# A sparse-attention block with two expert layers on one core: the rows of the next expert are split ahead of the weight conversion

## The chip, the cores and the metric

The kernel runs on one core of one Trainium2 chip. The metric is the device time of one execution in microseconds (us). The kernel before has a median of 1108.11 us over three runs (1107.55 to 1112.84). The core has five engines that each run their own instructions in order and meet through semaphores: TensorE (PE: matmuls; PEld is its weight load), VectorE (DVE), ScalarE (ACT), GpSimd (POOL) and SyncE (SP, which here only issues DMA transfers).

## The reference, cut to what matters

```python
x   = attention(q, k, v)             # 4 x 8 heads x 576 x 64, causal window 128, a bias by distance
x   = x.transpose(0, 2, 1, 3).reshape(2304, 512)
lg  = x @ w_gate + log1p(exp(x @ w_noise)) * noise      # 8 experts
top2, weight = the two largest of lg, softmax over them
for e in range(8):                   # layer 1: w1[e] 512 x 1024, w2[e] 1024 x 512
    rows = tokens that chose e
    out[rows] += weight * (relu(x[rows] @ w1[e]) @ w2[e])
h   = relu(out @ w_in)               # layer 2: w_in 512 x 2048, w_out 2048 x 512
return (h * h) @ w_out
```

All of it is float32. The kernel reaches that precision on PE by splitting a number into a high and a low part (type fp32r) and adding three products: high by high, high by low, low by high. So every operand of an expert matmul must be split on other engines first.

## The kernel before, in words

There are three stages: attention with the routing, the eight experts, and the second layer. The change lies in the experts and at the end of the first of them.

**Experts.** Each expert has at most 630 rows here, in five groups j = 0 to 4 (of 126 or 128 rows), and its weights come in eight blocks f = 0 to 7. A step n = 8e + f is one block of one expert. In PE's order a step is `expert_a(n)`, called a(n) here (12 matmuls into the PSUM tile hA, for the first 374 rows, then 12 into hB, for the rest), then `expert_b(n-1)`, called b(n-1) (15 matmuls that add the previous block to the five results y). T(n) is the time at which a(n) starts. hA has two PSUM buffers, hB has one, so hB of the next step waits until ACT and DVE have emptied this one. That emptying is `relu`: ACT writes the high part, then DVE writes the low part. The DVE half of it is called the relu below.

**What else a step does**, in the order of the code in `experts`:
- `fetch` lets POOL gather the rows of the next expert out of DRAM (group f, by row numbers in the tile `ids`), and lets SP transpose the group before it.
- `load_weights(n+7)` and `load_half(n)` are transfers on SP's queue, which runs in order. A half is one half of a block of the second layer's weights, in float64 bits that have to be made into float32.
- `begin_half` (ACT, line 1092) and `convert_half` (six DVE instructions, lines 1104 to 1109) convert the half that was loaded one step earlier. Together the six are called the conversion. The list HALVES names the steps that load one: 32 in all.
- `split_weights(n+5)`: ACT casts the high part of the weights (line 725, the cast), and POOL subtracts four pieces for the low part (line 729).
- `prepare` makes the next expert's operand: ACT joins two byte planes (line 427) and casts the high part (line 758), and DVE subtracts the low part (line 759, called the split below; the tile is `turned`). Group j is split in step f = j + 3, so group 4 is split in step f = 7, just ahead of the next expert's a.

The engines' order on PE, DVE, ACT and SP is the order of the code. POOL's is chosen by the scheduler, and it is the same in both kernels. The cast of w(n+5) writes into the buffers of w(n-1), so it starts when b(n-1) has ended, which is at T(n+1). Everything that `prepare` has on ACT stands behind that cast.

**Expert 0** is run in two passes (`first_expert`): the first over the 256 rows that are routed early, the second over the rest. In the second pass the rows of expert 1 are fetched and prepared. The row numbers of expert 0's late groups, of experts 1 to 6 and of expert 7 are loaded by three transfers in `settle`. Ahead of expert 1 stands a branch over code for more rows than planned (`overflow`, line 866); it is not taken with these inputs, and every engine jumps over that code.

## Time and profile before

| | |
|---|---|
| median of three runs | 1108.11 us (1107.55 to 1112.84) |
| the profiled execution | 1101.99 us |
| its span | 1100.2 us |
| PE busy in the span | 1036.5 us (94%) |
| DVE, ACT, POOL busy | 534.4, 485.2, 483.5 us (49%, 44%, 44%) |
| chain that ended last | PE 58%, DVE 5%, DMA 4%, issue 3%, POOL 2%, ACT 1% |
| attention and expert 0 | up to 283.3 us |
| experts 1 to 7 | from 283.3 to some 690 us |
| second layer | from there to the end |

PE is the engine to watch. An idle stretch of PE is printed behind the row that ends it, with the instruction that was waited for. [...] Idle time of the other engines matters only where PE waits at its end.

### The profile page before, as it was taken

The page shows a single profiled execution, that of the slowest core. Times are in us where ns is not written, and L with a number is a line of the kernel's source. Part 1 is how long each engine was busy: PE and PEld are TensorE (multiplying, and loading weights), DVE is VectorE, ACT ScalarE, POOL GpSimd, SP SyncE. Part 2 cuts the span into 40 slices and gives each one's busy share as a digit, 9 for nine tenths or more (in the row PEclk, how much of TensorE's full clock was granted, in tenths as well). Part 3 has the DMA queues.
Part 4 walks back from the last instruction along what each step waited for, and adds up shares of the span by engine and source line. Part 5 has one row for each costly group of instructions (what it writes and reads, how often), then busy time and mean ns, then how long its engine had stood idle before and what let it go on. Part 6 is the DMA issues. An engine that isn't in the chain of part 4 may idle for free.

```text
span 1100.2 us, 17058 instructions
## 1 busy us (share of the span) xinstructions
PE 1036.5 (94%) x6264; PEld 931.6 (85%) x6264; DVE 534.4 (49%) x1353; ACT 485.2 (44%) x897; POOL 483.5 (44%) x558
## 2 busy tenths in 40 slices
PE   4798989979899999998999999999999999999998
PEld 3687778869788989897888988899999999999997
DVE  7779687642357576756574421562232322223211
ACT  4678586435345454543453532553333333323322
POOL 5356464434466676665566563322222222222221
PEclk7879898789999999998999999999999999999999
DMA  9999993266495958586767422211212221031101
GB/s 200 173 177 207 192 170 102 79 151 158 129 208 172 212 185 215 192 216 188 185 170 199 113 67 72 72 39 34 73 20 67 48 68 39 10 83 33 29 1 29
DMA packets 204269, 131.43 MB, mean 119 GB/s; under 512 B 123108, under 2 KB 180580, under 8 KB 204176
## 3 DMA queue, kind: packets, MB, share of 16 engines
q1 hardware_dynamic: 195312, 109.39, 42.3%
q0 software_dynamic: 8864, 20.86, 6.9%
q8 instruction: 51, 0.84, 0.3%
q14 instruction: 42, 0.34, 0.1%
HBM read 84.56 MB, written 19.95 MB: 95 GB/s over the span
## 4 chain that ended last, share of the span: by engine, by line
PE 58%; DVE 5%; DMA 4%; issue 3%; POOL 2%; ACT 1%; SPq 0%; POOLq 0%; ACTq 0%; DVEq 0%
PE y L734 30%; PE h L734 18%; PE hA L734 6%; PE hB L734 5%; DMA raw<-in_moe_w_out_dram 2%; DVE turned L759 1%; POOL ring L729 1%; DMA y_dram<-xT,ids 1%; DVE raw L1108 1%; DVE store L1105 1%; DVE store L1106 1%; DMA raw<-in_moe_w_in_dram 1%; DVE raw L1107 1%; POOL first L729 0%; DVE hh L820 0%
## 5 line engine op out<-in xcount | busy, mean ns | idle before, releaser
L1141 POOL TENSOR_TENSOR hh<-relu,hh 128x384 fp32r<-128x384 f32 x96 | 97.2, 1013 | 296.9 <-ACT hh L1140 296.9
L1138 DVE SCALAR_TENSOR_TENSOR relu<-h,relu 128x384 f32<-128x384 f32 x96 | 53.5, 557 | 246.6 <-ACT relu L1137 246.6
L734 PE MATMUL y<-first,hh 128*126 128x512 f32 (+2 forms) x642 | 158.8, 396 | 0.0
L734 PE MATMUL y<-ring,hh 128*126 128x512 f32 (+1 forms) x612 | 151.7, 396 | 0.3 <-POOL hh L1141 0.3
L734 PEld LDWEIGHTS y<-first,hh 128*126 128x126 f32 (+2 forms) x642 | 117.7, 188 | 24.4 <-ACT hh L819 0.3
L734 PEld LDWEIGHTS y<-ring,hh 128*126 128x126 f32 (+1 forms) x612 | 112.9, 189 | 23.7 <-POOL hh L1141 0.8
L1137 ACT ACTIVATE relu<-h 128x384 f32<-128x384 f32 x96 | 47.1, 491 | 192.8 <-PE h L734 192.8
L729 POOL TENSOR_TENSOR first<-raw,first 128x256 fp32r<-128x256 f32 x116 | 97.0, 866 | 68.7 <-ACT first L725 55.6
L729 POOL TENSOR_TENSOR ring<-raw,ring 128x256 fp32r<-128x256 f32 x108 | 93.3, 893 | 52.1 <-ACT ring L725 41.7
L734 PE MATMUL y<-store,hh 128*128 128x512 f32 (+1 forms) x444 | 114.7, 397 | 0.0
L734 PE MATMUL h<-turned,store 128*128 128x384 f32 x552 | 107.4, 337 | 0.0
L734 PEld LDWEIGHTS h<-turned,store 128*128 128x128 f32 x552 | 98.1, 188 | 4.0
L734 PEld LDWEIGHTS y<-store,hh 128*128 128x128 f32 (+1 forms) x444 | 83.7, 190 | 15.3
L820 DVE SCALAR_TENSOR_TENSOR hh<-hA,hh 128x374 fp32r<-128x374 f32 (+3 forms) x76 | 39.8, 523 | 99.6 <-ACT hh L819 99.4
L734 PE MATMUL hA<-turned,first 128*128 128x374 f32 (+3 forms) x444 | 82.0, 335 | 4.2 <-ACTq L866 3.5
L734 PEld LDWEIGHTS hA<-turned,first 128*128 128x128 f32 x444 | 76.7, 194 | 7.9 <-ACTq L866 3.9
L1140 ACT CAST hh<-relu 128x384 fp32r<-128x384 f32 x96 | 49.3, 514 | 69.3 <-DVE relu L1138 65.5
L734 PE MATMUL hA<-turned,ring 128*128 128x374 f32 (+3 forms) x420 | 74.6, 327 | 0.0
L734 PEld LDWEIGHTS hA<-turned,ring 128*128 128x128 f32 x420 | 70.5, 188 | 3.0
L353 ACT ACTIVATE prob<-neg,least 128x256 f32<-128x256 f32 (+2 forms) x144 | 61.4, 473 | 9.3 <-DVE least L346 7.7
L759 DVE TENSOR_TENSOR turned<-x,turned 128x504 fp32r<-128x504 f32 (+2 forms) x41 | 41.1, 1004 | 47.3 <-ACT turned L758 47.1
L359 PE MATMUL ps_pt<-identf,prob 128*128 128x128 f32 (+1 forms) x256 | 49.2, 315 | 14.4 <-DVE den L408 11.4
(202 smaller groups left out, 1952.1 us busy)
## 6 DMA issues: line engine op xcount, KB each, us to landing
raw<-in_moe_w_dram SPq DMA_DIRECT2D x128, 256.0 KB, 3.7
raw<-y_dram SPq DMA_DIRECT2D x18, 512.0 KB, 4.0
raw<-in_moe_w_in_dram SPq DMA_DIRECT2D x16, 512.0 KB, 5.7
raw<-in_moe_w_out_dram SPq DMA_DIRECT2D x16, 512.0 KB, 5.8
vraw<-in_v_dram SPq DMA_DIRECT2D x36, 128.0 KB, 5.5
x_dram<-xn SPq DMA_DIRECT2D x18, 256.0 KB, 3.3
out_dram<-osb SPq DMA_DIRECT2D x36, 128.0 KB, 2.4
qraw<-in_q_dram SPq DMA_DIRECT2D x7, 512.0 KB, 4.9
```

What stands on the lines that cost most here:

```text
L353: self.nc.scalar.activation(u.p[:, a, :u.w], u.neg[:, a, :u.w], AF.Exp, bias=u.least[:, a:a + 1], scale=-1.0)
L359: self.nc.tensor.transpose(u.pt[:n, a, ci, :], u.p[:, a, ci * P:ci * P + n], self.identf)
L729: engine.tensor_sub(w[1][:, c], raw[:, c], w[0][:, c])
L734: self.nc.tensor.matmul(out, a(x), b(y), start=first and i == 0, stop=last and i == 2)
L759: self.nc.vector.tensor_sub(dst[:, 1, :, col:col + n], x[:, :, :n], dst[:, 0, :, col:col + n])
L820: nc.vector.scalar_tensor_tensor(hh[:, 1], ps, 0.0, hh[:, 0], op0=ALU.max, op1=ALU.subtract)
L1105: nc.vector.tensor_scalar(a, a, 3, 0x3FFFFFFF, op0=ALU.logical_shift_left, op1=ALU.bitwise_and)
L1106: nc.vector.scalar_tensor_tensor(a, hi, -0x40000000, a, op0=ALU.bitwise_and, op1=ALU.bitwise_or)
L1137: nc.scalar.activation(r, ps, AF.Relu)
L1138: nc.vector.scalar_tensor_tensor(r, ps, 0.0, r, op0=ALU.max, op1=ALU.mult)
L1140: nc.scalar.copy(hh[:, 0, :], r)
L1141: nc.gpsimd.tensor_sub(hh[:, 1, :], r, hh[:, 0, :])
```

## The change

Five edits: (1) HALVES leaves out the steps f = 7, so that no half is converted in the step f = 0, in which the five results of an expert are copied out; the list still has 32 entries, so it now reaches into expert 7 (steps 56 and 58 instead of ending at step 50). (2) In `experts`, `prepare` stands ahead of `convert_half`. (3) In `first_expert`, `fetch` stands at the head of the loop. (4) There `prepare` has a lag of two blocks and no longer three. (5) The row numbers of expert 0 have a tile of their own.

```diff
-HALVES = [n for n in range(8, 8 * NE) if n % 8 in (0, 2, 3, 5, 6, 7)][:32]
+HALVES = [n for n in range(8, 8 * NE) if n % 8 in (0, 2, 3, 5, 6)][:32]
...
-            in_offset=bass.IndirectOffsetOnAxis(ap=self.ids[:, e, j, 0:1], axis=0))
+            in_offset=bass.IndirectOffsetOnAxis(ap=self.ids_of(e)[:, j, 0:1], axis=0))
...
-        self.ids = self.const.tile([P, NE, 5, 2], I32, name="ids")
+        self.ids0 = self.const.tile([P, 5, 2], I32, name="ids0")
+        self.ids = self.const.tile([P, NE - 1, 5, 2], I32, name="ids")
...
+    def ids_of(self, e):
+        return self.ids[:, e - 1] if e else self.ids0
...
         for f in range(8):
+            self.fetch(1, f + 1)
             if f + 1 < 8:
                 self.expert_a(0, f + 1, (1,))
             self.expert_b(0, (f,), rest)
             if 8 + f < 14:
                 self.split_weights(8 + f, nc.vector if f < 2 else nc.gpsimd)
                 self.load_weights(8 + f + 3)
-            self.fetch(1, f + 1)
-            self.prepare(1, f + 1, 3)
+            self.prepare(1, f + 1)
...
+            if e + 1 < NE:
+                self.prepare(e + 1, f)
             if n - 1 in HALVES:
                 self.convert_half(HALVES.index(n - 1))
-            if e + 1 < NE:
-                self.prepare(e + 1, f)
```

DVE before, from the split of group 4 (step f = 7 of expert 1) to the copies of the results y in step f = 0 of expert 2; the split is the row `turned`, the conversion the six rows with `store` and `raw`:

```order
L759 TENSOR_TENSOR turned<-x,turned 128x4x126
L820 SCALAR_TENSOR_TENSOR hh<-hA,hh 128x374
L820 SCALAR_TENSOR_TENSOR hh<-hB,hh 128x256
L1104 TENSOR_SCALAR store<-store 128x512
L1105 TENSOR_SCALAR store<-store 128x512
L1106 SCALAR_TENSOR_TENSOR store<-raw_6064,store 128x512
L1107 TENSOR_SCALAR raw_6064<-store 128x512
L1108 SCALAR_TENSOR_TENSOR raw_6064<-raw_6064 128x512
L1109 TENSOR_TENSOR store<-store,raw_6064 128x512
L838 COPY xT<-y_5707 126x512
L838 COPY xT<-y_5715 126x512
```

DVE in the changed kernel, the same place (its lines 1108 to 1113 are the conversion):

```order
L759 TENSOR_TENSOR turned<-x,turned 128x4x126
L1108 TENSOR_SCALAR store<-store 128x512
L1109 TENSOR_SCALAR store<-store 128x512
L1110 SCALAR_TENSOR_TENSOR store<-raw_5997,store 128x512
L1111 TENSOR_SCALAR raw_5997<-store 128x512
L1112 SCALAR_TENSOR_TENSOR raw_5997<-raw_5997 128x512
L1113 TENSOR_TENSOR store<-store,raw_5997 128x512
L820 SCALAR_TENSOR_TENSOR hh<-hA,hh 128x374
L820 SCALAR_TENSOR_TENSOR hh<-hB,hh 128x256
L838 COPY xT<-y_5708 126x512
L838 COPY xT<-y_5716 126x512
```

The conversion that stood between the relu of step f = 0 and the copies is gone, and the one that stood ahead of the split now stands behind it, between the split and the relu of the next step.

SP before, in the second pass of expert 0: the transposes of expert 1's rows (`xT<-x`) among the loads of weights:

```order
L705 DMA raw<-in_moe_w_dram 128x4x128
L707 DMA raw<-in_moe_w_dram 128x512
L705 DMA raw<-in_moe_w_dram 128x4x128
L707 DMA raw<-in_moe_w_dram 128x512
L705 DMA raw<-in_moe_w_dram 128x4x128
L707 DMA raw<-in_moe_w_dram 128x512
L785 DMA_TRANSPOSE xT<-x 128x8x128
```

SP in the changed kernel, the same place:

```order
L705 DMA raw<-in_moe_w_dram 128x4x128
L707 DMA raw<-in_moe_w_dram 128x512
L705 DMA raw<-in_moe_w_dram 128x4x128
L707 DMA raw<-in_moe_w_dram 128x512
L785 DMA_TRANSPOSE xT<-x 128x8x128
L705 DMA raw<-in_moe_w_dram 128x4x128
L707 DMA raw<-in_moe_w_dram 128x512
```

Each of the five transposes moves ahead of one pair of loads.

POOL before, with the semaphores that each instruction waits for: the gathers of expert 0's three late groups and the first of expert 1's:

```order
L745 DMA x<-x_dram,ids 128x1024 [waits DMAHW4_49,DMAHW5_49,DMAHW3_49,DMAHW6_49,DMAHW2_49,DMASW6_49]
L745 DMA x<-x_dram,ids 128x1024 [waits DMASW7_49,PE_49,Pool_49]
L745 DMA x<-x_dram,ids 128x1024 [waits DMASW0_49,PE_49]
L745 DMA x<-x_dram,ids 128x1024 [waits DMASW7_49,DMAHW4_49,DMASW1_49,Activation_49]
L745 DMA x<-x_dram,ids 128x1024 [waits DMASW2_49,DVE_49,PE_49]
```

POOL in the changed kernel, the same place:

```order
L745 DMA x<-x_dram,ids_3135 128x1024 [waits DMAHW4_49,DMAHW5_49,DMAHW3_49,DMAHW6_49,DMAHW2_49,DMASW6_49]
L745 DMA x<-x_dram,ids_3135 128x1024 [waits DMASW7_49,PE_49,Pool_49]
L745 DMA x<-x_dram,ids_3135 128x1024 [waits DMASW0_49,PE_49]
L745 DMA x<-x_dram,ids 128x1024 [waits DMASW7_49,DMAHW4_49,DMASW1_49,Activation_49]
L745 DMA x<-x_dram,ids 128x1024 [waits DMASW2_49,DVE_49,PE_49]
```

Only the name of the tile differs; the semaphores are the same, and so are the values that are waited for in the two programs.

## Rows read from the trace of the kernel before

**Rows 1.** Busy time by stretch (experts 1 to 7; after step 40's stall): PE, PEld, DVE, ACT, POOL, clock, DMA

```profile
283.34:690.00 406.66, 395.61 (x2182) 355.30 (x2183) 219.28 (x349) 182.58 (x279) 242.19 (x273) 0.98 0.62 168
...
519.62:523.00 3.38, 3.38 (x14) 3.18 (x15) 0.61 (x2) 0.62 (x2) 0.96 (x1) 0.50 0.69 200
```

**Rows 2.** Timeline of PE, expert 1: start, duration, instruction, [idle before it <- releaser]

```profile
316.35 2.22 PE L734 MATMUL hA<-turned,ring 128*128 128x374 f32 x12
321.03 2.21 PE L734 MATMUL hB<-turned,ring 128*128 128x256 f32 x12 [2.46 <-DVE hh L820]
327.64 2.22 PE L734 MATMUL hA<-turned,first 128*128 128x374 f32 x12
329.70 1.60 PE L734 MATMUL hB<-turned,first 128*128 128x256 f32 x12
334.61 2.22 PE L734 MATMUL hA<-turned,first 128*128 128x374 f32 x12
...
344.51 1.59 PE L734 MATMUL hB<-turned,first 128*128 128x256 f32 x11 [0.59 <-DVE turned L759]
```

**Rows 3.** Timeline of PE, first steps of experts 4 and 5 (32 and 40)

```profile
458.37 1.58 PE L734 MATMUL hB<-turned,first 128*128 128x256 f32 x11 [1.30 <-DVE turned L759]
...
511.84 2.23 PE L734 MATMUL hA<-turned,first 128*128 128x374 f32 x12
...
519.62 2.72 PE L734 MATMUL hB<-turned,first 128*128 128x256 f32 x11 [5.44 <-DVE turned L759]
526.18 2.22 PE L734 MATMUL hA<-turned,ring 128*128 128x374 f32 x12
```

**Rows 4.** Timeline of all engines, one step (14) of expert 1

```profile
327.66 1.05 ACT L725 CAST ring<-raw 128x1024 fp32r<-128x1024 f32 x1 [4.00 <-PE y L734]
...
328.79 3.29 POOL L729 TENSOR_TENSOR ring<-raw,ring 128x256 fp32r<-128x256 f32 x4 [0.36 <-ACT ring L725]
...
329.84 0.60 ACT L758 CAST turned<-x 128x504 fp32r<-128x504 f32 x1
...
330.48 1.00 DVE L759 TENSOR_TENSOR turned<-x,turned 128x504 fp32r<-128x504 f32 x1 [2.49 <-ACT turned L758]
...
331.85 0.41 DVE L820 SCALAR_TENSOR_TENSOR hh<-hB,hh 128x256 fp32r<-128x256 f32 x1
...
332.31 0.43 DVE L1104 TENSOR_SCALAR store<-store 128x512 f32<-128x512 f32 x1
...
335.38 0.69 DVE L1109 TENSOR_TENSOR store<-store,raw 128x512 f32<-128x512 f32 x1
```

**Rows 5.** The split by its line, steps 11 to 63: ns min/median/max, first and last start

```profile
L759 DVE TENSOR_TENSOR turned<-x,turned x30: 676/1203/1231, 319.0 to 632.9; 128x504 fp32r<-128x504 f32 x25, 128x512 fp32r<-128x512 f32 x4, 128x472 fp32r<-128x472 f32 x1
```

**Rows 6.** Timeline of ACT, step 12 of expert 1

```profile
313.56 0.66 ACT L1092 ACTIVATE store<-raw 128x512 f32<-128x512 f32 x1 [4.87 <-DMA raw<-in_moe_w_out_dram]
...
316.30 0.60 ACT L758 CAST turned<-x 128x504 fp32r<-128x504 f32 x1
```

**Rows 7.** Timeline of ACT, DVE and POOL, step 40 (first of expert 5)

```profile
512.80 0.61 ACT L758 CAST turned<-x 128x504 fp32r<-128x504 f32 x1
...
513.15 3.18 DVE L1105 TENSOR_SCALAR store<-store 128x512 int32<-128x512 int32 x1
513.26 2.79 POOL L729 TENSOR_TENSOR first<-raw,first 128x256 fp32r<-128x256 f32 x4
```

**Rows 8.** The branch line 866: instructions by engine's queue, ns min/median/max, first and last start

```profile
L866 ACTq EVENT_SEMAPHORE  x2: 17/17/17, 283.3 to 283.4; - x2
...
L866 PEldq COMPARE_BRANCH  x1: 4625/4625/4625, 278.4 to 278.4; - x1
```

**Rows 9.** Timeline around the branch: PE, POOL, ACT

```profile
281.14 0.99 POOL L839 DMA_INDIRECT y_dram<-xT,ids  x1 [3.27 <-ACT xT L838]
281.23 0.62 ACT L758 CAST turned<-x 128x504 fp32r<-128x504 f32 x1
...
283.34 3.21 PE L734 MATMUL hA<-turned,first 128*128 128x374 f32 x12 [3.49 <-ACTq L866]
```

More of the change, by code (lines that the diff above doesn't have):

```diff
@@ L840, in expert_b @@
                     out=self.y_dram[:, :],
-                    out_offset=bass.IndirectOffsetOnAxis(ap=self.ids[:n, e, j, 1:2], axis=0),
+                    out_offset=bass.IndirectOffsetOnAxis(ap=self.ids_of(e)[:n, j, 1:2], axis=0),
                     in_=ysb[:n], in_offset=None)
@@ L914, in load_ids @@
         rows = self.ids_dram[e * REG + j0 * P:e * REG + j1 * P, :]
-        self.nc.sync.dma_start(self.ids[:, e, j0:j1], rows.rearrange("(j p) o -> p j o", p=P))
+        self.nc.sync.dma_start(self.ids_of(e)[:, j0:j1], rows.rearrange("(j p) o -> p j o", p=P))
+    def ids_of(self, e):
+        return self.ids[:, e - 1] if e else self.ids0
     def early_rows(self):
@@ L965, in settle @@
         src = self.ids_dram.rearrange("(e r) o -> e (r o)", e=NE)[1:NE - 1, :10 * P]
-        nc.sync.dma_start(self.ids[:, 1:NE - 1].rearrange("p e j o -> p e (j o)"),
+        nc.sync.dma_start(self.ids[:, :NE - 2].rearrange("p e j o -> p e (j o)"),
                           src.rearrange("e (p a) -> p e a", a=10))
```

## The prediction

> **What bounds the kernel now.** I read busy time by stretch first. In experts 1 to 7 PE works 395.61 of 406.66 us [rows 1], so at most 11.05 us of idle time can be won there, and whatever the slow clock costs behind a long stall; what comes after is the same code in both kernels. The timeline of PE then says where those 11 us lie. An undisturbed step lasts 334.61 - 327.64 = 6.97 us, and its hB starts 2.06 us after T [rows 2]. Stalls are few, and DVE ends all of them but one. In the first step of an expert PE stops after one matmul of hB and waits for the split of group 4: 0.59 us in step 16 [rows 2], 1.30 in step 32 and 5.44 in step 40 [rows 3]; the first steps of experts 3 and 6 have a row like that of step 16. In step 13 hB waits 2.46 us for the relu of step 12 [rows 2]. [...] The exception stands ahead of expert 1, where PE is idle for 3.49 us until line 866 on ACT's queue [rows 9].
>
> Then I read one quiet step engine by engine [rows 4], with T(14) = 327.64. ACT's cast starts at T, because it waits for PE's b. The high part of the next expert's group is there at T + 2.80 (329.84 + 0.60), the split runs from T + 2.84 to T + 3.84, the relu of hB ends at T + 4.62, and the conversion runs from T + 4.67 to T + 8.43 (3.76 us). The deadline of the relu is the next hB, at T + 6.97 + 2.06 = T + 9.03. So before, the relu has 4.4 us to spare.
>
> **Expert 0's row numbers apart: 0 us.** The gathers wait for the same semaphores at the same values in both programs. The wait that the edit would remove is not there, because the regions of the tile were already told apart.
>
> **Expert 1's rows a step sooner: 0 us for PE, something for POOL.** The gap ahead of expert 1 ends with the jump. PE's compare-and-branch starts at 278.4 and lasts 4625 ns, to 283.0, and ACT's own semaphore rows of that line stand at 283.3 [rows 8]. The last row work on ACT ended at 281.23 + 0.62 = 281.85, before either [rows 9]. When it goes, the jump is late next, and it does not move, because PE's order ahead of it is the same; I take 0 (bounds 0 and 4.5, the second in the rivals). On SP five transposes pass one pair of loads each. The gathered rows they wait for come from POOL instructions that stand far ahead, and the loads behind them wait for a free buffer anyway, so this costs nothing; were a gather late, loads for expert 1's blocks would be late with it. On POOL there is a gain: the scatter of expert 0's results waited 3.27 us for copies on ACT [rows 9] that stand behind a join and a cast for expert 1's rows, which are now done a step earlier. A cast is 0.6 us [rows 9] and the join ahead of it starts with the cast of weights and ends with this one: from 327.66 + 1.05 to 329.84 is 1.1 us at least [rows 4]. So POOL leaves expert 0 some 1.7 us earlier.
>
> [...]
>
> **The split ahead of the conversion.** The split cannot start before ACT's high part, at T + 2.80. Before, DVE used the wait for it to convert. Now the conversion stands behind the split, and the relu behind the conversion. From the same rows: split to T + 3.84, conversion 3.87 + 3.76 = T + 7.63, both relus (331.48 to 332.26, 0.8) to T + 8.4. That is 0.6 us ahead of the deadline where there were 4.4. This holds for four steps in each of six experts (a split followed by a conversion, f = 3, 4, 6, 7): 24 steps. Price of one: 0 if the conversion takes 3.76. POOL's pieces end at 328.79 + 3.29 = T + 4.44, inside the new place of the conversion, and DVE instructions beside POOL are longer: the split takes 676 ns at least and 1203 in the median [rows 5]. One instruction lengthened by 0.5 uses up nearly all of the slack; with all six it would be overdrawn by 2.4. I take 0.1 for each, +2.4 us (bounds 0 and 12, at 0.5 each).
>
> *First steps.* The high part of group 4 is there 512.80 + 0.61 - 511.84 = 1.57 us after T [rows 7, 3], a split beside POOL takes 1.2 [rows 5], and the second matmul of hB would start at T + 2.33. So about 0.5 us of stall stays even with a free DVE, and steps 16, 24 and 48 have no more than that now: 0. Step 32 goes from 1.30 to 0.6: -0.7. Step 56, which had almost no conversions ahead of it, gets them now: +0.5 (bounds 0 and 0.7).
>
> *Step 40.* Ahead of its split stood a conversion in which one instruction took 3.18 us, until POOL's four pieces had ended (513.26 + 2.79 = 516.05) [rows 7]. That conversion now stands behind the split. What delays the split still is the conversion of the step before, which waits for its own split: in step 12, rows of the same kind show the high part ready at 316.90, 2.7 us behind the end of ACT's first part of the conversion, 314.22 [rows 6]. If the late half comes again, I put the stall at 2.2 us and the loss at 3.5: -3.9. Without it the loss is 0.8: -6.6. I take -3.9, since a late transfer of this kind is in the trace.
>
> *Step 13.* This is the opposite case. The half came 4.87 us late, ACT finished its part at 314.22, and the high part of the split followed at 316.90 [rows 6]. DVE could convert in between; now it waits. That is 2.7 us longer for the relu that PE waits for, less the 1.7 by which POOL is earlier: +1.0 (bounds -4.3, the whole loss of 11.29 - 6.97 [rows 2], and +2.7).
>
> **The halves of f = 7 left out.** The six instructions that stood between the relu of f = 0 and the copies go, 3.76 us of DVE. PE did not wait for them. Their place is taken by the conversion from behind the split. 32 conversions stay 32; the last ones move into experts 6 and 7, where PE waits for nothing of theirs: 0.
>
> **Sum.** 0 + 0 + 2.4 - 0.7 + 0.5 - 3.9 + 1.0 = -0.7 us, against the profiled execution's 1101.99 (span 1100.2): 1101.3. The timed median is 1108.11, 6.1 us above the profiled execution, and the same difference gives 1107.4. I predict 1107 us: no change. About 0.5% (5.5 us) is what a measurement of this kernel can tell from none.
>
> **Rivals.**
>
> *Faster: the stalls that DVE ends go.* Speaks for it: a split no longer stands behind a slow conversion, and there is one conversion fewer around the copies. Against it: 0.5 us of each first step is ACT's, and the relu pays. Step 40 -6.6, step 32 -0.7, step 13 wholly gone -4.3, no price in the 24 steps, +0.5: -11; two thirds of it, as some late transfers return: about 1100.5 us. Chance 0.23.
>
> *Faster: the rows, not the jump, hold PE ahead of expert 1.* Then PE goes on at once: 3.49 us, and the first hA at its usual length, 3.21 - 2.22 = 1.0 [rows 9, 2]: -4.5, with the -0.7 about 1103 us. For it: the gap's releaser is printed as ACT. Against it: PE's own branch row. [...] Chance 0.06.
>
> *Slower: the relu becomes the bound.* The mechanism is one: a conversion beside POOL is longer than 4.4 us (9.03 - 3.87 - 0.8), so the relu ends behind T + 9.03, and hB of the next step waits, in up to 24 steps. For it: the slack of 0.6 us, and a split that is usually at its long duration. Against it: POOL's pieces end 0.6 us into the conversion in rows 4. At 0.5 us each it is +12, less 3 of the gains: +9, about 1117 us; it decides from 0.3 us each. Chance 0.21.
>
> [...]
>
> **How the numbers follow.** No change 0.50, the rivals 0.23, 0.06 and 0.21. The branch case lies at the edge of what can be told, so I count it as faster by half: faster 0.27, same 0.52, slower 0.21. The forecast's own range is 1103 to 1112. To hold 8 in 10 it must reach well into both sides: 1099 to 1116.
>
> **What would show it.** In the changed kernel's trace: PE's branch row still some 4.6 us and the gap ahead of expert 1 within 0.3 of 3.49; the split starting right behind ACT's cast and the conversion behind it; the relu of hB ending near T + 8.4 in steps f = 4, 5, 7 and 0; first steps at 0.5 to 0.8 us of stall; step 40 below 3. It is wrong if hB waits for the relu in many steps (slower), if the waits for `turned` all go (faster), or if the gap ahead of expert 1 closes.

## The result and the profile after

The changed kernel takes 1097.07 us in the median of 20 runs (1091.3 to 1105.1), against 1107.69 us for the kernel before on the same chip (20 runs). The ratio is 0.9909, with a 95% interval of 0.9885 to 0.9934: some 10 us faster. The forecast was no change at 1107 us, with a range of 1099 to 1116, so the time fell outside the range on the fast side. What came true is the rival "the stalls that DVE ends go", which was put at 1100.5 us, nearer to its whole sum of -11 us than to the two thirds of it that it took.

The profiled execution took 1095.01 us (span 1093.3, granted clock 0.966 as a share of full speed), 6.98 us less than that of before. Experts 1 to 6, from the first hA of step 8 to that of step 56, are called the stretch below. It went from 631.35 - 283.34 = 348.01 us to 623.75 - 288.23 = 335.52 us: -12.49. Most of the difference to 6.98 lies ahead of the stretch, which began 4.89 us later in this execution. Two executions of either kernel differ as much there (288.23 and 283.69 us in the changed kernel, 283.34 and 292.41 in the one before), so these 4.89 us can't be put down to the change. I compare stretches below, each from one profiled execution, and give the ratio of timed runs beside them.

Busy time in the stretch, of the kernel before and of the changed one (columns as in [rows 1]):

```profile
283.34:631.35 348.01, 337.02 (x1857) 303.30 (x1858) 207.11 (x327) 164.58 (x248) 216.94 (x241) 0.98 0.69 183
288.23:623.75 335.52, 334.36 (x1857) 300.56 (x1858) 186.44 (x306) 163.44 (x246) 202.89 (x239) 0.99 0.66 186
```

In the stretch PE now idles for 335.52 - 334.36 = 1.16 us, where it was 348.01 - 337.02 = 10.99. Of the 12.49 us 9.83 are idle time, and 2.66 are matmuls that took less time (mean granted clock 0.99 instead of 0.98). The timeline of PE shows which stalls went (start, duration, instruction, idle time before it and its releaser):

```profile
288.23 3.26 PE L734 MATMUL hA<-turned,first 128*128 128x374 f32 x12 [3.85 <-ACTq L866]
...
323.66 1.70 PE L734 MATMUL hB<-turned,ring 128*128 128x256 f32 x12 [0.19 <-DVE hh L820]
...
345.11 1.59 PE L734 MATMUL hB<-turned,first 128*128 128x256 f32 x11 [0.16 <-DVE turned L759]
...
513.53 1.57 PE L734 MATMUL hB<-turned,first 128*128 128x256 f32 x11 [0.15 <-DVE turned L759]
```

They answer to [rows 9], [rows 2] (steps 13 and 16) and [rows 3] (step 40). The wait in step 13 fell from 2.46 to 0.19 us, that in step 40 from 5.44 to 0.15, and every first step now waits 0.15 or 0.16. Only the gap ahead of expert 1 stayed. There the rows of the branch line answer to [rows 8]:

```profile
L866 ACTq EVENT_SEMAPHORE  x2: 17/17/17, 288.2 to 288.2; - x2
L866 PEldq COMPARE_BRANCH  x1: 4685/4685/4685, 282.9 to 282.9; - x1
```

Last, one step with a split and a conversion (step 28, T = 426.97), from the timelines of ACT, DVE and PE; it answers to [rows 4]:

```profile
429.27 0.60 ACT L758 CAST turned<-x 128x504 fp32r<-128x504 f32 x1
...
429.90 0.98 DVE L759 TENSOR_TENSOR turned<-x,turned 128x504 fp32r<-128x504 f32 x1 [5.36 <-ACT turned L758]
430.81 0.96 DVE L1108 TENSOR_SCALAR store<-store 128x512 f32<-128x512 f32 x1
...
434.18 0.69 DVE L1113 TENSOR_TENSOR store<-store,raw 128x512 f32<-128x512 f32 x1
434.79 0.54 DVE L820 SCALAR_TENSOR_TENSOR hh<-hA,hh 128x374 fp32r<-128x374 f32 x1
435.25 0.41 DVE L820 SCALAR_TENSOR_TENSOR hh<-hB,hh 128x256 fp32r<-128x256 f32 x1
...
436.01 1.60 PE L734 MATMUL hB<-turned,ring 128*128 128x256 f32 x12
```

This is the order that the prediction walked: high part, split, conversion, relus. Of the six conversion instructions only the first, beside POOL's pieces (they end at 431.48), is long (0.96 where it takes 0.43 alone). The relu ends at 435.66 = T + 8.69, 0.35 us ahead of the hB at 436.01, which does not wait.

### The profile page after: what moved, and what is told of

Read it like the earlier page. It is cut to its first block, busy times and chain, and to the rows that moved or that the text cites. A ratio compares the mean times of both kernels' runs of the same rounds, so it can differ in the third digit from the quotient of the medians.

```text
span 1093.3 us, 17064 instructions
## 1 busy us (share of the span) xinstructions
PE 1033.5 (95%) x6264; PEld 927.8 (85%) x6264; DVE 526.7 (48%) x1353; ACT 483.8 (44%) x897; POOL 472.7 (43%) x558
## 4 chain that ended last, share of the span: by engine, by line
PE 61%; DVE 4%; issue 4%; ACT 2%; DMA 1%; POOL 1%; SPq 0%; ACTq 0%; POOLq 0%
PE y L734 31%; PE h L734 18%; PE hA L734 7%; PE hB L734 6%; DVE turned L759 1%; ACT x L427 1%; DMA y_dram<-xT,ids 1%; DVE store L1108 1%; DVE hh L820 1%; DVE raw L1112 1%; DVE store L1110 1%; DMA raw<-in_moe_w_out_dram 0%; ACT turned L758 0%; DVE raw L1111 0%; DVE store L1109 0%
## 5 line engine op out<-in xcount | busy, mean ns | idle before, releaser
L729 POOL TENSOR_TENSOR first<-raw,first 128x256 fp32r<-128x256 f32 x116 | 92.1, 824 | 73.3 <-ACT first L725 68.6
L729 POOL TENSOR_TENSOR ring<-raw,ring 128x256 fp32r<-128x256 f32 x108 | 85.4, 822 | 60.0 <-ACT ring L725 57.4
L759 DVE TENSOR_TENSOR turned<-x,turned 128x504 fp32r<-128x504 f32 (+2 forms) x41 | 37.9, 926 | 90.3 <-ACT turned L758 90.1
```

Source lines behind the costliest of these rows:

```text
L729: engine.tensor_sub(w[1][:, c], raw[:, c], w[0][:, c])
L759: self.nc.vector.tensor_sub(dst[:, 1, :, col:col + n], x[:, :, :n], dst[:, 0, :, col:col + n])
```

## Experiments

"Stretch" is the time from the first hA of step 8 to that of step 56, in the profiled execution of each kernel. Ratios are against the kernel before, timed on the same chip.

| kernel | stretch, us | ratio (95%) |
|---|---|---|
| before, two executions | 348.01, 352.76 | 1 |
| changed, two executions | 335.52, 337.57 | 0.9909 (0.9885 to 0.9934), 0.9921 (0.9882 to 0.9960) |
| e2: order alone | 356.58 | 1.0101 (1.0068 to 1.0135) |
| e3: list of halves alone | 344.79 | 0.9963 (0.9919 to 1.0007) |
| e4: first expert alone | 344.53 | 0.9977 (0.9939 to 1.0015) |
| e5: order and list | 340.18 | 0.9972 (0.9935 to 1.0009) |
| e6: order, copies ahead | 352.48 | 1.0043 (1.0010 to 1.0076) |
| e7: changed, no branch | 333.65 | 0.9867 (0.9816 to 0.9918) |
| e8: changed, branch moved | 334.54 | 0.9888 (0.9827 to 0.9950) |
| e9: order and list without f = 6 | 339.86 | 1.0041 (0.9998 to 1.0083) |
| e10: e6, halves asked for first | 336.69 | 0.9941 (0.9904 to 0.9977) |
| e11: changed, longer conversion | 363.47 | 1.0156 (1.0083 to 1.0230) |
| e12: e8, halves asked for first | 332.91 | 0.9877 (0.9818 to 0.9937) |
| e13: order, halves asked for first | 350.81 | 1.0051 (1.0011 to 1.0091) |
| e14: before, halves asked for first | 335.21 | 0.9872 (0.9816 to 0.9928) |

### e1: the kernel before, profiled again

> The kernel before, unchanged, profiled a second time. The stretch from the first expert_a of expert 1 to that of expert 7 took 348.0 us before (283.34 to 631.35) and 335.5 in the changed kernel. Theory A (habit): steps 13 and 40 stall in every execution, since late halves are part of the schedule: the stretch again takes 346 to 350 us, with a wait of hB over 2 us in at least one step. Theory B (accident): the two long stalls were of that one execution: the stretch takes 338 to 341 us, and only the 0.5 to 0.7 us waits in first steps are left, so half of the gain seen in the two traces is chance.

Measured: 1116.03 us, stretch 352.76, longer than either theory had it. It is a single run near the top of this kernel's times on that chip (1099.48 to 1117.31), so its length counts for little; which steps wait is what is read from it. Two first steps of PE's timeline, of experts 2 and 3:

```profile
354.69 2.72 PE L734 MATMUL hB<-turned,first 128*128 128x256 f32 x11 [4.09 <-DVE turned L759]
...
414.34 1.71 PE L734 MATMUL hB<-turned,ring 128*128 128x256 f32 x11 [2.56 <-DVE turned L759]
```

In the first execution these two steps waited 0.59 and 0.66 us, and step 40 waited 5.44. The stalls are a habit, as theory A had it, but their place and size change from one execution to the next (e3 and e4, which have the same order, show it too). So something that varies feeds them, and it wasn't right to forecast them one by one from one execution.

### e2, e3, e4: the parts of the change alone

e2 only swaps `prepare` and `convert_half`:

```diff
+            if e + 1 < NE:
+                self.prepare(e + 1, f)
             if n - 1 in HALVES:
                 self.convert_half(HALVES.index(n - 1))
-            if e + 1 < NE:
-                self.prepare(e + 1, f)
```

> Only the order of split and conversion is changed (prepare ahead of convert_half); the list of halves and expert 0 are as before. Theory 1 (the order does it): the split of group 4 starts right behind ACT's cast, first steps wait 0.2 us instead of 0.5 to 5.4, the stretch of experts 1 to 6 takes 336 to 338 us, ratio to before 0.990 to 0.993. Theory 2 (the list does it): with a conversion left in the step where the results are copied, the relu of that step waits behind two conversions; hB waits for the relu near the first steps, stretch 343 us or more, ratio 0.997 to 1.003.

Measured: slower than before by 1%. The first steps wait 0.16 us for the split, but PE's timeline has new waits in their place:

```profile
325.45 2.93 PE L734 MATMUL hB<-turned,ring 128*128 128x256 f32 x12 [5.10 <-DVE hh L820]
...
360.01 4.60 PE L734 MATMUL y<-first,hh 128*126 128x512 f32 x12 [2.15 <-DVE xT L838]
```

The second row comes back in five experts (2.12 to 2.23 us): the new expert's y waits until DVE has copied out the old one's. Neither theory had this wait.

e3 only takes f = 7 out of the list:

```diff
-HALVES = [n for n in range(8, 8 * NE) if n % 8 in (0, 2, 3, 5, 6, 7)][:32]
+HALVES = [n for n in range(8, 8 * NE) if n % 8 in (0, 2, 3, 5, 6)][:32]
```

> Only the list of halves is changed (none at f = 7). Theory 1 (the order does it): the split of group 4 still stands behind the conversion of f = 6, so first steps still wait 0.5 to 1.3 us for it; stretch of experts 1 to 6 342 to 346 us, ratio 0.996 to 1.000. Theory 2 (the list does it): fewer transfers and conversions where results leave, the late halves are gone; stretch 336 to 339 us, ratio 0.990 to 0.994.

Measured: not to be told from before, as theory 1 had it. The waits for `turned` in the first steps stay (1.35, 0.63, 0.39, 3.29, 0.36 us), and step 13 waits 3.58 for the relu.

e4 has the edits on expert 0's row numbers (`ids_of`) and on expert 1's rows alone:

```diff
         for f in range(8):
+            self.fetch(1, f + 1)
...
-            self.fetch(1, f + 1)
-            self.prepare(1, f + 1, 3)
+            self.prepare(1, f + 1)
```

> Only expert 0's edits: row numbers apart, expert 1's rows a step sooner. Theory 1 and 2 alike: nothing that PE waits for changes; the gap ahead of expert 1 stays at 3.3 to 3.9 us and the late gathers of expert 0 still cost 5.3 us; ratio 0.997 to 1.002. Theory 3 (POOL is released earlier and the transfers of expert 1 come sooner): the 2.5 us stall of step 13 goes, with its slow clock 4 us in all, ratio 0.995 to 0.997.

Measured: not to be told from before by the time. In the rows theory 3 holds: step 13 waits no more, but the first steps do (1.29, 0.35, 1.29, 2.64, 2.42). The three ratios multiply to 1.004, and the whole change has 0.991. No part alone has the gain; it lies in how they meet.

### e5: order and list together

The changed kernel without the edits of e4.

> The changed order and the shorter list of halves together, without the changes to expert 0's row numbers and expert 1's rows. Alone the order gave a ratio of 1.0101 and the list 0.9963, the other part 0.9977, and all together 0.9909. Theory P (pair): the order gains only when no conversion stands ahead of the copies of results, so the pair gives nearly all: ratio 0.991 to 0.994, every first step (from its hA to the next step's) 7.4 us, no wait of y for the copies of line 838, first steps wait for the split 0.2 us at most. Step 13 may still lose 2 to 4 us, because POOL leaves expert 0 later. Theory F (first expert): the parts multiply, so without the edits on expert 1's rows the pair gives only the product of the two, 1.0064, and the gain comes from those edits in the new order.

Measured: stretch 340.18, every first step 7.36 to 7.39 us, no wait for the copies. That is theory P in the rows, with the reservation that it made: in step 13

```profile
317.10 2.93 PE L734 MATMUL hB<-turned,ring 128*128 128x256 f32 x12 [2.18 <-DVE hh L820]
```

so that step takes 10.89 us instead of 7.43, which is 3.5 of the 4.7 us by which this stretch is longer than the changed kernel's. Theory F's 1.0064 lies outside the interval of the ratio (0.9935 to 1.0009). But so does P's 0.991, and 0.994 stands at its edge: the time suggests that the edits of e4 have a share of their own. It doesn't show it, since the interval of the changed kernel's second series (0.9882 to 0.9960, e15) overlaps this one.

### e6 and e10: copies ahead of the conversion, then halves asked for earlier

e6 is e2 with the conversion behind the copies in an expert's first step:

```diff
-            if n - 1 in HALVES:
+            if n - 1 in HALVES and f:
                 self.convert_half(HALVES.index(n - 1))
...
                 self.expert_b(e, (f,), range(3 if e == last and f in late else 5))
+            if n - 1 in HALVES and f == 7:
+                self.convert_half(HALVES.index(n - 1))
```

> The changed order alone, with the full list of halves, but in the code of an expert's first step the conversion stands behind the copies of results (line 838) instead of ahead of them. The order alone gave 1118.96 us, with y waiting 2.1 to 2.2 us for these copies in five experts (steps of 9.35 to 11.0 us instead of 7.0). Theory C (copies): the conversion ahead of the copies is the whole loss; the y waits fall below 0.3 us, 12 to 16 us go, ratio 0.995 to 0.999. Rival D (too much work on DVE in those steps): the loss moves to the relu behind the conversion, which now has two copies ahead of it as well; hB waits 0.5 to 2.5 us for hh in five steps, and the ratio stays above 1.003.

Measured: the waits of y are gone, but only 4 us of the stretch with them. Timelines of ACT and PE, in step 20 (T = 379.76) and in step 21 behind it, the expert's sixth (T = 386.69):

```profile
381.40 0.66 ACT L1094 ACTIVATE store<-raw 128x512 f32<-128x512 f32 x1 [4.53 <-DMA raw<-in_moe_w_out_dram]
...
391.98 1.22 PE L734 MATMUL hB<-turned,first 128*128 128x256 f32 x8 [3.08 <-DVE hh L820]
```

The wait for the relu that rival D named is there, but not where D put it (five first steps). It is in the sixth step of each expert, and ACT's row says why: a half landed 4.53 us late. ACT's cast and high part stand behind that instruction, the split behind the high part, the conversion behind the split, the relu behind the conversion. Both theories missed that.

e10 is e6 with two statements swapped, so that SP asks for a half ahead of the step's two weight loads:

```diff
+            if n in HALVES:
+                self.load_half(HALVES.index(n))
             if n + 7 < 8 * NE and n + 7 not in self.raw:
                 self.load_weights(n + 7)
-            if n in HALVES:
-                self.load_half(HALVES.index(n))
```

> As the order with the copies ahead of the conversion and the full list (1.0043), but on SP's queue a half is asked for ahead of the step's two weight loads instead of behind them. There hB waited for the relu in step 13 and in the sixth step of five experts (5.00, 3.08, 0.38, 1.47, 0.46, 2.21 us), each time where ACT had waited 3.3 to 4.5 us for a half to land. Theory L (late halves): the half lands about 2 us earlier (512 KB of weights at some 200 GB/s), ACT's waits for it go below 2 us, the waits of hB go except perhaps that of step 13, -6 to -10 us: ratio 0.996 to 0.999. Rival W: the weights that are now behind come late instead, or the transfers share the engines so that nothing lands earlier; ratio 1.003 to 1.006.

Measured: stretch 336.69, 15.8 us shorter by this swap. hB waits for the relu twice (1.51 and 1.07 us, steps 13 and 53). One cast waited 2.9 us for its weights and still began with its step. Theory L holds.

### e9 and e13: what the copies wait for

e9 is e5 with another half left out:

```diff
-HALVES = [n for n in range(8, 8 * NE) if n % 8 in (0, 2, 3, 5, 6)][:32]
+HALVES = [n for n in range(8, 8 * NE) if n % 8 in (0, 2, 3, 5, 7)][:32]
```

> As the pair (order and shorter list, 0.9972), but the list leaves out the halves of f = 6 instead of f = 7: as many halves for an expert, as many transfers, but a conversion again ahead of the copies of results. Theory C (copies): it matters which half is left out; y waits some 2.1 us for the copies of line 838 in the step behind each first step, five times 2 to 2.5 us over the pair: ratio 1.006 to 1.009. Rival N (number of halves): only the number matters, because fewer transfers are late; ratio 0.997, no y waits above 0.5 us.

Measured: no wait of y, stretch 339.86 as in e5 (340.18). In the rows theory C in this form falls: it doesn't matter which of the two halves goes. The ratio (1.0041) speaks the other way: its interval (0.9998 to 1.0083) holds C's 1.006 and leaves out rival N's 0.997, though it overlaps e5's. The profiled execution was the fastest of the twelve (1086.82 us, median 1099.97), and its rows have nothing that would cost the difference; where it comes from stays open.

e13 is e2 with the swap of e10.

> The changed order alone with the full list (1.0101; from the first hA of expert 1 to that of expert 7 it took 356.58 us, against 348.01 before and 335.52 in the changed kernel), and each half asked for ahead of the step's weights. Theory L (late halves decide): the stretch falls to 337 to 341 us and the ratio to 0.993 to 0.997. Theory C (two conversions ahead of the copies of line 838): y still waits some 2 us in five steps and the steps behind the first ones stay at 9 to 11 us; the stretch stays at 348 or more, the ratio at 1.000 or more.

Measured: y waits 2.08 to 2.16 us in five steps, ratio above 1, though ACT waits for halves only 5.4 us in all. PE's and DVE's timelines around the first of them:

```profile
339.13 0.82 DVE L759 TENSOR_TENSOR turned<-x,turned 128x504 fp32r<-128x504 f32 x1
339.88 0.96 DVE L1104 TENSOR_SCALAR store<-store 128x512 f32<-128x512 f32 x1
...
345.50 0.42 DVE L1104 TENSOR_SCALAR store<-store 128x512 f32<-128x512 f32 x1
...
350.63 1.27 DVE L838 COPY xT<-y 126x512 f32<-126x512 f32 x2
...
351.37 4.62 PE L734 MATMUL y<-first,hh 128*126 128x512 f32 x12 [2.14 <-DVE xT L838]
```

Between the last split of an expert and the copies stand two conversions (two rows of line 1104), the halves of f = 6 and f = 7, and each takes some 5 us here. With one of them, as in e9 and in the changed kernel, the copies are in time. So the shorter list was needed because the order moved a conversion into that place.

### e14: the kernel before, with the halves asked for earlier

The swap of e10 and nothing else.

> The kernel before with nothing changed but that each half is asked for ahead of the step's weights. Theory O (the order is needed): the first steps of the experts still wait for the split, 0.5 us or more in at least three of them, because a conversion stands ahead of it; the stretch from expert 1 to expert 7 stays at 342 us or more, ratio 0.994 to 1.000. Rival L (late halves made those stalls too): waits at 0.2 us, stretch below 338 us, ratio 0.990 to 0.993.

Measured: the rival. The stretch is as short as the changed kernel's, and the first steps wait 0.17 us at most, with the old order and the full list:

```profile
328.13 1.72 PE L734 MATMUL hB<-turned,ring 128*128 128x256 f32 x12 [0.59 <-DVE hh L820]
349.63 1.58 PE L734 MATMUL hB<-turned,first 128*128 128x256 f32 x11 [0.17 <-DVE turned L759]
```

So the stalls of the kernel before came from halves that landed late. Its own trace has the chain of the longest of them, that of step 40 (T = 511.84), in the rows of ACT and DVE:

```profile
505.34 0.67 ACT L1092 ACTIVATE store<-raw 128x512 f32<-128x512 f32 x1 [3.32 <-DMA raw<-in_moe_w_out_dram]
506.04 0.43 DVE L1104 TENSOR_SCALAR store<-store 128x512 f32<-128x512 f32 x1 [3.47 <-ACT store L1092]
...
510.77 1.22 DVE L759 TENSOR_TENSOR turned<-x,turned 128x504 fp32r<-128x504 f32 x1
...
518.89 0.68 DVE L759 TENSOR_TENSOR turned<-x,turned 128x504 fp32r<-128x504 f32 x1
```

A half came 3.32 us late a step earlier. The conversion at the head of DVE's queue waited for it, so that conversion, the split behind it (510.77) and the relus all came late. The next conversion then began only at 512.71, met POOL's pieces (the 3.18 us instruction of [rows 7]), and the split of group 4 behind it started at 518.89. In e14 the same conversion, in the same order, has no such instruction (the longest takes 0.69 us), and that split waits only for ACT (0.38 us). The view of line 1092 (the conversion's first part, on ACT) tells it in two lists: what ACT waited for ahead of it, and who waited for it (us, times). In the kernel before:

```profile
  DMA raw<-in_moe_w_out_dram: 25.7, 12
  DMA raw<-in_moe_w_in_dram: 1.3, 3
...
  DVE store L1104: 30.0, 17
```

In e14:

```profile
  DMA raw<-in_moe_w_out_dram: 8.6, 6
  DMA raw<-in_moe_w_in_dram: 1.5, 1
...
  DVE store L1104: 9.9, 6
```

And in the changed kernel (its line 1096):

```profile
  DMA raw<-in_moe_w_in_dram: 10.8, 7
  DMA raw<-in_moe_w_out_dram: 9.0, 7
...
  DVE store L1108: 2.7, 4
```

In e14 the halves land earlier. In the changed kernel ACT still waits 19.8 us for halves, but DVE waits for ACT's part of the conversion only 2.7 us. It doesn't wait less in all: its waits for the high part that the split needs grow from 34.0 to 77.2 us (from the start of expert 1 to 640 us). But no split stands behind a late conversion any more. In the two steps ahead of each first step halves are also less late than they were, by 0.84 us at most (1.03 in e15) where it was 3.32. One link back to the transfers stands in the waits for line 759: POOL's gathers waited for the split 12.8 us (11 times) before, 2.5 us (twice) in e14 and 0.3 us (once) in the changed kernel, and SP's weight loads, which have the half behind them, wait for POOL (118.8 us in 36 waits of line 705 before, from the start of expert 1 to that of expert 7). What share of the gain runs through this link was not measured. Two cures for one cause.

### e11: how much room the relu has

```diff
         nc.vector.tensor_scalar(af, af, 2.0 ** -15, None, op0=ALU.max)
+        nc.vector.tensor_scalar(af, af, 2.0 ** -15, None, op0=ALU.max)
+        nc.vector.tensor_scalar(af, af, 2.0 ** -15, None, op0=ALU.max)
```

> The changed kernel with the first instruction of a conversion given three times (the maximum with a constant, so the values stay): 2 x 0.43 us more on DVE in each conversion. This measures the slack of the relu. In the changed kernel a relu of hB behind a split and a conversion ends at T + 8.6, and hB is due at T + 9.03. Theory S (slack of 0.4 us): 0.86 us is 0.43 too many, hB waits about that in each of some 24 steps: +10 us over the changed kernel, ratio 1.000. Rival Z (DVE has room, the deadline as walked is not the true one): hB waits in fewer than six steps, ratio 0.991 to 0.993.

Measured: +27.95 us of stretch, far more than theory S had. Timelines of DVE and PE in a first step (32, T = 454.72):

```profile
455.95 1.22 DVE L1115 TENSOR_TENSOR store<-store,raw 128x512 f32<-128x512 f32 x1
...
457.55 0.41 DVE L820 SCALAR_TENSOR_TENSOR hh<-hB,hh 128x256 fp32r<-128x256 f32 x1
...
458.10 0.35 PE L734 MATMUL hB<-turned,first 128*128 128x256 f32 x1 [1.17 <-DVE hh L820]
...
459.05 1.23 PE L734 MATMUL hB<-turned,first 128*128 128x256 f32 x8 [0.59 <-DVE turned L759]
```

The 0.86 us more push the conversion's last instruction to 455.95 = T + 1.23, where in step 28 of the changed kernel POOL's pieces began (428.20 = T + 1.23), and there it takes 1.22 instead of 0.69 us; the relu is 1.17 late, the split behind it as well. hB waits once for each pair of neighbouring conversions (the sixth step and the first), not in all 24 steps, but dearer each time: against the changed kernel 1.2 to 1.3 us in the sixth steps of four experts, 1.8 to 3.4 in the first steps, where the waits come twice, and 3.4 and 5.7 in steps 13 and 53, where a half was late as well. So the room ahead of the bound is real and below 0.86 us, as the "slower" rival said; the changed kernel just stays inside it.

### e7, e8, e12: the branch

e7 is the changed kernel without the branch:

```diff
-            if n == 8:
-                self.overflow()
```

> The changed kernel without the branch of line 866 (the code for more rows than planned is left out; these inputs never take it). In the changed kernel PE is idle for 3.85 us there and the first hA takes 3.26 instead of 2.2 us. Theory J (jump): the gap closes to under 0.5 us and the first hA is at its usual 2.2: -4.5 us, ratio 0.9865 against before. Rival R (rows): something else is as late, the rows of expert 1 or POOL; a gap of 2 us or more stays with another releaser, and the ratio stays at 0.990.

e8 moves it, and gives the weight tiles of the code behind it another buffer (not printed here):

```diff
                 while self.side or self.routes:
                     self.run_side()
+                for _, relu in self.put_off:
+                    relu()
+                self.put_off = []
+                self.overflow()
                 for j in rest:
...
-            if n == 8:
-                self.overflow()
```

> The changed kernel with the branch moved ahead of the join of expert 0's late rows, where PE is idle for 5.49 + 1.37 us anyway (244.12 and 246.60 in its trace), and with the two weight tiles of the code behind the branch in another buffer. Theory J: the jump lies in that idle time, the gap ahead of expert 1 closes (under 0.5 us), the idle time ahead of the late rows stays within 1 us of 6.9: -4.5 us, ratio 0.9865 against before, which would beat both kernels. Rival K: DVE and ACT jump as well, and the joins of the late rows stand behind their jumps, so the idle time there grows by 3 to 4.5 us and nothing is won: ratio 0.990.

Measured, PE's timeline of e8:

```profile
245.17 2.98 PE L754 MATMUL x<-identf,x 128*128 128x128 f32 x12 [5.10 <-DVE x L427]
...
283.40 3.35 PE L734 MATMUL y<-store,hh 128*128 128x512 f32 x9 [1.65 <-ACT hh L819]
286.55 3.14 PE L734 MATMUL hA<-turned,first 128*128 128x374 f32 x12
```

Moved, the jump costs nothing (the idle time ahead of the late rows is 5.10 where it was 6.86), and it doesn't stand ahead of expert 1 any more. But a second wait was hidden under it: ACT's relu of expert 0's last block, behind the rows of expert 1, 1.65 us here, 2.29 in e7 and 2.15 in e12. From expert 0's last hA to the hA of step 10 it is 22.30 us in the changed kernel, 21.16 in e7 and 20.48 in e8: 1.1 and 1.8 us won instead of 4.5. Each theory was half right.

e12 adds the swap of e10 to e8.

> The changed kernel with the branch moved to expert 0's late rows (0.9888) and a half asked for ahead of the step's weights. What is left there to win: waits of hB for the relu (0.43 us in one step) and the 1.65 us ahead of expert 1. If late halves decide (theory L), no hB wait for hh is left; at most 1 us is won, ratio 0.987 to 0.989, not to be told from 0.9888 by the median, only by the rows. Rival W: weights land late, hA waits for them in some steps, ratio 0.990 or more.

Measured: stretch 332.91, the shortest, no wait of hB for the relu at all, no cast that waits for weights, and ACT waits 5.1 us for halves in all. It beats the kernel before, clear of the noise (0.9877, 0.9818 to 0.9937). By its rows it beats the changed kernel by some 2.6 us; the intervals of the two ratios overlap, so the time does not show that.

### e15: the changed kernel, profiled again

> The changed kernel unchanged, a second look. If what its first profile shows is a habit of the program, the first steps wait 0.2 us or less for the split again, the stretch from expert 1 to expert 7 is 335 to 337 us, and the ratio to before is 0.988 to 0.994. If that profile was a lucky one, stalls of 0.5 us and more come back in some first steps or in the sixth steps, as they moved about in the two profiles of before (348.01 and 352.76 us).

Measured: 0.9921, stretch 337.57. The first steps wait 0.16 us at most again; step 13 waits 1.28 and step 53 1.05 us for the relu where ACT had waited 3.7 and 3.5 us for a half. The gain is a habit, and what is left of late halves still shows, in the sixth steps that the expectation named.

## Why the prediction was wrong

The stretch came out 12.5 us shorter, where the sum without step 56, which lies behind it, said 1.2. Step by step, in the profiled executions:

| step of the prediction | forecast | measured |
|---|---|---|
| split ahead, 24 steps | +2.4 | +0.6 (step 53 +0.49, step 37 +0.13) |
| steps 16, 24, 48 | 0 | -0.44, -0.54, -0.37 |
| step 32 | -0.7 | -1.15 |
| step 40 | -3.9 | -6.97 |
| step 13 | +1.0 | -3.86 |
| step 56 | +0.5 | 0.0 |
| branch, row numbers | 0 | gap ahead of expert 1 from 3.49 to 3.85 |

**The step that failed is that of the late transfers**, in "Step 40" and "Step 13": "If the late half comes again", and "That is 2.7 us longer for the relu". I saw the late half in [rows 6] and treated it as two events that would come back, and as a cost of the new order. e14 shows that late halves were the cause of the long stalls altogether. In the kernel before DVE waits for ACT's part of a conversion at the head of its queue, 17 times and 30.0 us in all, with the split queued behind; the prediction had no row of that list, and it would have told that -3.9 and -6.6 belong to the same mechanism as the 0.5 to 1.3 us of the other first steps. Both are counted from what step 40 lost before, less the 3.5 and the 0.8 us that the prediction left it: the step took 526.18 - 511.84 = 14.34 us [rows 3] where an undisturbed one takes 6.97 [rows 2], 7.37 too many. Of these 5.44 are the stall and 1.93 came on top, with a granted clock of 0.50 just behind it [rows 1].

In the changed kernel no half was 0.3 us late in the two steps ahead of step 40, so the condition of -3.9 was not met. In step 13 the sign was wrong, and the traces say which term. Take the time behind T(12) at which ACT begins with the half, and the wait of hB in step 13:

| kernel | order | half, us behind T(12) | hB waits, us |
|---|---|---|---|
| before | old | 4.17 | 2.46 |
| e1 | old | 3.12 | 1.43 |
| e3 | old | 5.29 | 3.58 |
| e14 | old | 2.28 | 0.59 |
| e4 | old | -0.80 | 0 |
| e2 | new | 3.85 | 5.10 |
| e5 | new | 1.74 | 2.18 |
| e9 | new | 1.39 | 1.82 |
| e13 | new | 0.53 | 1.07 |
| e15 | new | 0.85 | 1.28 |
| changed | new | 0.21 | 0.19 |

In the old order hB waits 1.7 us less than this time (not at all in e4), in the new one as long or up to 1.3 us longer. So the new order does cost this step: 1.7 to 3.0 us for the same half, where 2.7 were walked. What was mis-sized is "less the 1.7 by which POOL is earlier". The half came 3.96 us earlier in its step than before, and in e4, which has the edits of the first expert alone, 4.97 us. The request of this half in the kernel before (T(12) = 309.39; its ACT row is in [rows 6]):

```profile
306.48 0.43 SPq L1084 DMA_DIRECT2D raw<-in_moe_w_out_dram  x1
```

Its request and ACT row in the changed kernel (T(12) = 314.26):

```profile
309.37 0.47 SPq L1088 DMA_DIRECT2D raw<-in_moe_w_out_dram  x1
...
314.47 0.66 ACT L1096 ACTIVATE store<-raw 128x512 f32<-128x512 f32 x1 [3.03 <-DMA raw<-in_moe_w_out_dram]
```

It was asked for 1.98 us earlier (T(12) - 4.89 instead of T(12) - 2.91), and ACT began with it 5.10 us behind the request instead of 7.08. The first is near what the prediction gave to POOL: the first gather of expert 1's stage starts 11.00 us behind T(8) in the changed kernel and 13.29 before, 2.3 us where 1.7 were forecast, and SP's transposes, which wait for gathers (15.9 us in two waits ahead of this request before, 14.4 in one in the changed kernel), stand ahead of that request. The shorter way had no term; why it was shorter was not measured, nor the share of earlier rows and of POOL's release apart.

**The first steps.** "about 0.5 us of stall stays even with a free DVE" was too large: 0.15 to 0.16 stayed. The split was taken at the 1.2 us it has beside POOL [rows 5]. In a first step it took 0.81 in the changed kernel, and the wait was 0.17 even in the old order of e14.

**The price of 24 steps.** The mechanism was right, and the size 0.1 was too much: where no half is late, the walked end of the relu, T + 8.4, was T + 8.6 to T + 8.7, still ahead of T + 9.03, and such a step has no price at all until the room is used up. e11 shows the cliff behind it. In the rows of step 28 an instruction beside POOL's pieces took 0.96 us instead of 0.43, in those of e11 one that ran where these pieces are due 1.22 instead of 0.69. The 1.22 us row has two inputs, the 0.96 us row and the 3.18 us row of [rows 7] have one. And in step 28 one instruction of six was longer, not all: POOL's pieces had ended (431.48) when the second began.

**The halves of f = 7 left out: "0".** Alone that is right (e3: 0.9963, the interval holds 1). With the new order it is worth 16.4 us of stretch between e2 (356.58) and the pair of e5 (340.18), of which some 15 lie in the five steps behind the first ones, because a second conversion ahead of the copies costs more than 2 us in each of five experts (e2, e13). The prediction priced the edits one at a time and had no term for their meeting, although its own order rows showed the conversion moving into the place ahead of the copies.

**Right were** the jump ahead of expert 1 (PE's branch row 4685 ns, the gap 3.85 us) and the order of the steady step. The gap is 0.36 us longer than before, a little more than the 0.3 allowed for it, and e7 shows that the price of 4.5 us in the branch rival was too high: without the jump 1.1 us were won, as ACT's relu was nearly as late. The zero for the row numbers was not tested by itself; they changed only together with expert 1's rows (e4). The chance of 0.23 for the rival that came true was too small mainly for one reason: "two thirds of it, as some late transfers return" was an argument about the transfers, and no row behind it had been followed to its cause.

## What to carry to other kernels

Ask of every late transfer who waits for the instruction that waits for it: a list of waiters on a minor engine (30.0 us behind a 0.66 us instruction) can explain stalls three queues further on, and moving one DMA request ahead of two others (e14) can then be worth as much as a new order of work. Where stalls of one kind differ in size between executions, forecast their cause and not each of them. And price edits of one queue together: an order that pushes work ahead of something urgent is good or bad by what another edit takes out of that place.

## What the runs showed of the hardware that was not expected

- With the jump over code that is not taken ahead of expert 1, PE was idle there for 3.36 to 3.85 us in two executions of the kernel before, two of the changed one, and in e2, e6, e13 and e14. Moved to a place where PE idles anyway (5.49 + 1.37 us in the changed kernel; the join that ends the first had waited 5.19 us for a gather), it cost nothing that shows (5.10 us in e8).
- Asked for ahead of 512 KB of weights instead of behind them, halves of 512 KB made ACT wait 10.1 us instead of 27.0 in all, and no cast waited for weights (e14). Rows of SP and ACT for the same half (third block of expert 2), in step 19: in e1 it was asked for 1.5 us behind the step's start (374.73) and had landed at 381.81,

```profile
374.61 0.99 SPq L705 DMA_DIRECT2D raw<-in_moe_w_dram  x1
375.64 0.53 SPq L707 DMA_DIRECT2D raw<-in_moe_w_dram  x1
376.22 0.43 SPq L1084 DMA_DIRECT2D raw<-in_moe_w_out_dram  x1
...
381.81 0.67 ACT L1092 ACTIVATE store<-raw 128x512 f32<-128x512 f32 x1 [3.03 <-DMA raw<-in_moe_w_out_dram]
```

  in e14 0.2 us behind it (368.39), landing at 373.68:

```profile
368.59 0.57 SPq L1084 DMA_DIRECT2D raw<-in_moe_w_out_dram  x1
369.27 0.40 SPq L705 DMA_DIRECT2D raw<-in_moe_w_dram  x1
...
373.68 0.67 ACT L1092 ACTIVATE store<-raw 128x512 f32<-128x512 f32 x1 [1.24 <-DMA raw<-in_moe_w_out_dram]
```

  Of the 1.8 us by which it came earlier in its step, 1.3 are the earlier request and 0.5 a shorter way.
- Two stalls of one length cost differently in e2, with the clock behind them: the twelve matmuls behind the 2.15 us wait of y took 4.60 us at a granted clock of 0.63, those behind the 2.14 us wait an expert later 3.03 us at 1.00.
